# Threshold attention and GELU feed-forward on one core: score slots by query half, and the weight conversion's sign in a step of its own

## The chip, the cores and the metric

The kernel runs on one NeuronCore of a Trainium2 chip. The metric is the device time of one execution in microseconds (us). The five queues that matter are PE (matmul, with PEld for its weight loads), DVE (the vector engine), ACT (the scalar engine), POOL (GpSimd) and SP (issues nearly all DMAs).

## What is computed

Attention over 8 batches x 8 heads, 576 positions, head size 64, with a threshold per row, then a feed-forward block on the 4608 rows of 512 values:

```python
scores = scale * q @ k.T
thresh = max(scores, axis=-1) - tau
scores = where(scores >= thresh, scores, -1e9)
attn = exp(scores - max(scores)); attn /= sum(attn) + 1e-9
x = (attn @ v) rearranged to (B*S, H*D)
h = x @ w_in                      # 512 x 2048
out = (h / (1 + exp(-1.702 * h))) @ w_out   # 2048 x 512
```

The inputs q, k, v are float32. The two weight matrices arrive as float64, so the kernel makes float32 of them itself.

## The kernel before

**Pairs.** Two heads make a pair; there are 32 pairs, n = 0 to 31, four to a batch. The scores are kept transposed: keys on partitions, queries along the row. A pair has four main tiles of 128 keys for each head (t = 0 to 3) and one tail tile (t = 4) with the last 64 keys of both heads. `load_qk` and `load_v` (lines 183 to 207) bring q, k, v; `prep` (279) transposes q and k on DVE; `scores` (294) makes the scores of a tile on PE; `keep` (315) copies them from PSUM to an SBUF tile on ACT; `in_groups` (330) takes maxima over blocks on DVE; `over_tiles`, `over_groups`, `lower` and `spread_max` make the threshold of every query and spread it; `sub` (381) subtracts it on DVE; `mask` and `exps` (391, 395) follow on ACT; `values` (416) multiplies with v on PE; `sums_by_pe` (425, pairs 0 to 7) makes the denominators on PE, for later pairs DVE sums; `spread_sums` and `place_x` put the normalised result into `xT`.

**PSUM.** The pool `psA` has three slots of [128, 2, 512] float32. A main tile of scores takes two slots at once, one for each head; the two places in a slot hold the two halves of 288 queries. PE issues four matmul calls, half by half and head by head, each with 64 rows of the array; every call appears as two MATMUL records of 288 columns. Then two copies of [128, 576] follow, one for each head. The tail takes one slot, and so does `values`, from its start to `place_x`. The pool `psM` (two slots) serves the feed-forward block.

**Feed-forward.** Rows come in 9 blocks of 512. For each block there are 32 tasks `mm1` (line 490) and 32 tasks `mm2` (line 509), each two matmul calls, so four MATMUL records. `tanh` (ACT) and `gelu` (DVE, 501) follow every second `mm1`. Pair n may start its scores only after feed-forward task 16 (n - 6), so that the attention of later pairs runs among the feed-forward work of earlier ones.

**Weight conversion.** The weights come in 64 pieces of 128 x 256, 32 for w_in and 32 for w_out. `load_w` (215) issues two DMAs for a piece, the 64-bit words and the same bytes shifted by three. `cv_open` (233) is three DVE instructions: the fraction bits masked (239), the sign put into the fraction by an arithmetic shift and an exclusive or (243), the exponent field (248). `cv_mant` (254) turns the fraction into a float on ACT; `cv_exp` (259) clamps and shifts the exponent in two POOL instructions (262, 265); `cv_end` (269) multiplies both on POOL (272) and writes the float32 weight. The first feed-forward block waits for the pieces that each of its tasks reads.

**The order.** No engine chooses at run time. `run_in_order` (115) lists all tasks beforehand: each task has an engine, a cost in us, a rank, what it comes after, which buffers it takes and gives back, and a lag until others see its end. Whenever an engine is free, the ready task of lowest rank whose buffers are free goes next. The instructions are issued in that order, and the hardware then waits on semaphores with its own durations. Attention tasks of pair n have rank n, feed-forward matmuls 1000, `tanh`, `gelu` and the output tasks -1, conversion tasks 3.2 + i/64. The planner's costs and buffers for a piece are

```python
a = task("SP", 1.1, rank, load_w, i, take=("w64",), lag=3.5)
a = task("DVE", 1.0, rank, cv_open, i, after=[a], take=("cv",), give=("w64",))
m = task("ACT", 0.42, rank, cv_mant, i, after=[a])
e = task("POOL", 1.0, rank, cv_exp, i, after=[a])
ready_w.append(task("POOL", 0.9, rank, cv_end, i, after=[e, m], give=("cv",)))
```

with three buffers `w64` and two `cv`. For a main tile of scores they are 1.2 (PE), twice 0.64 (ACT, rank n) and 1.37 (DVE); a `mm1` or `mm2` costs 1.8, a `sub` 1.37, a `gelu` 0.7, `values` 5.0.

Of the kernel before, what the change touches and what calls it, by code (L numbers as in the profile page):

```python
# [9 lines left out]

FP32 = mybir.dt.float32
I32 = mybir.dt.int32
U32 = mybir.dt.uint32
U8 = mybir.dt.uint8
AF = mybir.ActivationFunctionType
ALU = mybir.AluOpType
# [3 lines left out]
P = 128  # L20
# [10 lines left out]
def kernel(  # L31
# [29 lines left out]
    nc = tc.nc  # L61
    B, H, S, D = q.shape
# [5 lines left out]
    SH = S // 2  # L68
# [11 lines left out]
    work = ctx.enter_context(tc.tile_pool(name="work", bufs=2))  # L80
    psA = ctx.enter_context(tc.tile_pool(name="psA", bufs=3, space=bass.MemoryType.PSUM))
# [6 lines left out]
    kd = [const.tile([P, P], FP32, name=f"kd{i}") for i in range(2)]  # L88
# [21 lines left out]
    def task(engine, cost, rank, f, *a, after=(), take=(), give=(), lag=0.06):  # L110
        tasks.append((engine, cost, rank, f, a, [x for x in after if x is not None],
                      take, give, lag))
        return len(tasks) - 1
# [57 lines left out]
    def home(n, tag, size, name, bufs, key=None):  # L171
        if n in APART:
            o = offset[key or tag]
            return spare[:, o : o + size]
        return work.tile([P, size], FP32, name=name, tag=tag, bufs=bufs)

    def own(n, *pools):
        return tuple(x + "_apart" for x in pools) if n in APART else pools
# [30 lines left out]
    WC = 256  # L209
# [3 lines left out]
    cv = {}  # L213
# [18 lines left out]

    def cv_open(i):
        t, t3 = cv[i]
        hi = t[:, :, 1]


        frac = work.tile([P, WC], I32, name="frac", tag="frac")
        nc.vector.tensor_scalar(  # L239
            out=frac, in0=t3[:, :, 0].bitcast(I32), scalar1=0x0FFFFFFF, scalar2=0x10000000,  # L240
            op0=ALU.bitwise_and, op1=ALU.bitwise_or,
        )
        nc.vector.scalar_tensor_tensor(  # L243
            out=frac, in0=hi.bitcast(I32), scalar=31, in1=frac,
            op0=ALU.arith_shift_right, op1=ALU.bitwise_xor,
        )
        ex = work.tile([P, WC], U32, name="ex", tag="ex")
        nc.vector.tensor_scalar(  # L248
            out=ex, in0=hi, scalar1=20, scalar2=0x7FF,
            op0=ALU.logical_shift_right, op1=ALU.bitwise_and,  # L250
        )
        cv[i] = [frac, ex]

    def cv_mant(i):
        mant = work.tile([P, WC], FP32, name="mant", tag="mant")
        nc.scalar.activation(out=mant, in_=cv[i][0], func=AF.Copy, scale=2.0**-28)  # L256
        cv[i][0] = mant

    def cv_exp(i):

        ex = cv[i][1]
        nc.gpsimd.tensor_scalar(  # L262
            out=ex, in0=ex, scalar1=1150.0, scalar2=896.0, op0=ALU.min, op1=ALU.max
        )
        nc.gpsimd.tensor_scalar(
            out=ex, in0=ex, scalar1=-896.0, scalar2=2.0**23, op0=ALU.add, op1=ALU.mult
        )

    def cv_end(i):
        dst, _, c, j = pieces[i]  # L270
        mant, ex = cv.pop(i)
        nc.gpsimd.tensor_tensor(  # L272
            out=dst[:, c, ts(j, WC)], in0=mant, in1=ex.bitcast(FP32), op=ALU.mult
        )


    mats, sT, stats, mbs, pss = {}, {}, {}, {}, {}
# [13 lines left out]
    def halves(ap):  # L291
        return ap.rearrange("p (c s) -> p c s", c=2)

    def scores(n, t):
        qT, kT = mats[n, 0], mats[n, 1]
        if t == NKT:
            ps = [psA.tile([P, 2, 512], FP32, name="ps", tag="ps")]
            for c in range(2):
                nc.tensor.matmul(  # L299
                    ps[0][:, c, 0:SH], lhsT=kd[n % 2], rhs=qT[:, ts(c, SH)],  # L300
                    start=True, stop=True,
                )
            del mats[n, 0], mats[n, 1]
        else:
            ps = [psA.tile([P, 2, 512], FP32, name="ps", tag="ps") for _ in range(2)]
            for c in range(2):
                for h in range(2):
                    nc.tensor.matmul(  # L308
                        ps[h][:, c, 0:SH],
                        lhsT=kT[ts(h, D), ts(t, P)], rhs=qT[ts(h, D), ts(c, SH)],  # L310
                        start=True, stop=True,
                    )
        pss[n, t] = ps

    def keep(n, t, h):
        ps = pss[n, t][h]
        if t == NKT:
            st = work.tile([P, S], FP32, name="s_t", tag="s_t", bufs=2)
            o = st
        else:  # L320
            if h == 0:
                st = home(n, "s_m", 2 * S, "s_m", 7, f"s_m{t}")
                st = st.rearrange("p (h s) -> p h s", h=2)
            else:
                st = sT[n, t]
            o = st[:, h, :]
        sT[n, t] = st
        nc.scalar.copy(out=halves(o), in_=ps[:, :, 0:SH])  # L328

    def in_groups(n, t, op):  # L330

# [186 lines left out]
    def store(blk, i):  # L518
# [6 lines left out]
        out=tau_b, in_=bass.AP(tensor=tau.tensor, offset=tau.offset, ap=[[0, P], [1, 1]])  # L525
# [23 lines left out]

    FIRST, LAST = -1.0, 1000.0
    BY_PE = 8
    LEAD = 6

    ready_w = []
    for i in range(len(pieces)):
        rank = NPAIR - 0.8 + i / len(pieces)
        if not wide:
            ready_w.append(task("SP", 0.6, rank, load_w, i, lag=2.5))  # L560
            continue
        a = task("SP", 1.1, rank, load_w, i, take=("w64",), lag=3.5)
        a = task("DVE", 1.0, rank, cv_open, i, after=[a], take=("cv",), give=("w64",))
        m = task("ACT", 0.42, rank, cv_mant, i, after=[a])
        e = task("POOL", 1.0, rank, cv_exp, i, after=[a])
        ready_w.append(task("POOL", 0.9, rank, cv_end, i, after=[e, m], give=("cv",)))

    tau_done = task("DVE", 1.0, -2.0, tau_terms)

# [41 lines left out]
    for n in range(NP):  # L611
        gate = per_pair * (n - LEAD)
        after = ffn[gate : gate + 1] if gate >= 0 else []
        r = float(n)
# [4 lines left out]
        pq = task("DVE", 0.78, r, prep, n, 0, after=[lq], take=own(n, "qkT0"), give=own(n, "raw0"))  # L619
        pk = task("DVE", 0.78, r, prep, n, 1, after=[lk], take=own(n, "qkT1"), give=own(n, "raw1"))  # L620
        pd = task("ACT", 0.5, r, prep_kd, n, after=[pk])
        mx = []
        for t in range(NKT + 1):
            tail = t == NKT
            a = task(
                "PE", 1.1 if tail else 1.2, r, scores, n, t,
                after=[pq, pk] + ([pd] if tail else []) + after,
                take=("psA", "s_t") if tail else ("psA", "psA") + own(n, "s_m"),
                give=own(n, "qkT0", "qkT1") if tail else (),
            )  # L630
            after = [a]
            c = [
                task("ACT", 0.64, r, keep, n, t, h, after=[a], give=("psA",))
                for h in range(1 if tail else 2)
            ]
            mx.append(task("DVE", 0.78 if tail else 1.37, r, in_groups, n, t, ALU.max, after=c))
        a = task("DVE", 0.75, r, over_tiles, n, ALU.max, after=mx)
        a = task("DVE", 0.75, r, over_groups, n, ALU.max, after=[a])
        a = task("DVE", 0.6, r, lower, n, after=[a, tau_done])
        m = task("DVE", 1.38, r, spread_max, n, after=[a], take=own(n, "mb"))  # L640
        ws, subs = [], [m]
        for t in range(NKT + 1):
            tail = t == NKT
            a = task(
                "DVE", 1.5 if tail else 1.37, r, sub, n, t, after=subs[-1:],
                give=own(n, "mb") if tail else (),
            )
            subs.append(a)
            a = task("ACT", 0.7 if tail else 1.17, r, mask, n, t, after=[a])
# [3 lines left out]
        if n < NPAIR:  # L653

            pv = den = None
            for t in every:
# [3 lines left out]
                    take=("psM", "psM") if first else (),  # L660
# [3 lines left out]
                    take=("psA",) if first else (), give=(back[t],) if t < NKT else ("s_t", "v_m"),  # L664
                )
            a = task("DVE", 1.2, r, one_row, n, after=[den], give=("psM", "psM"))
        else:
            pv = task("PE", 5.0, r, values, n, every, after=ws + [lv], take=("psA",), give=("v_m",))
        if NPAIR <= n < BY_PE:
            a = task("PE", 5.2, r, sums_by_pe, n, every, False, after=ws + [pv], take=("psA",), give=back)  # L670
            a = task("DVE", 1.2, r, one_row, n, after=[a], give=("psA",))
        elif n >= BY_PE:
# [4 lines left out]
            a = task("DVE", 0.75, r, over_tiles, n, ALU.add, after=su + [pv], give=back)  # L677
            a = task("DVE", 0.75, r, over_groups, n, ALU.add, after=[a])
            a = task("DVE", 0.7, r, one_group, n, after=[a])
        a = task("DVE", 1.05, r, spread_sums, n, after=[a])  # L680
# [41 lines left out]
```

## Time and profile before

| | us |
|---|---|
| median of three runs | 1481.49 |
| lowest, highest | 1479.97, 1481.97 |
| the profiled execution | 1479.97 |
| its span (first to last instruction) | 1478.2 |
| PE busy | 1417.4 (96%) |
| DVE busy | 988.5 (67%) |
| ACT busy | 662.2 (45%) |
| POOL busy | 113.2 (8%) |

The profile is one execution. Its parts are: the busy time of each engine; the span in 40 slices with the busy share of each engine in tenths; the DMA queues; the chain of waits that ended last, followed back from the end; and groups of instructions by line, engine and shape. A group's line gives its count after an x, then busy us and the mean ns of one, then the idle time of the engine just before them and what ended it. A timeline or the chain in order of time begins each line with the start in us and the length in us. A busy PE is not PE at its peak, since matmuls overlap.

### The profile page before, as it was taken

To read this page: it belongs to the slowest core of one execution; us is meant where nothing else is said; L and a number is where in the kernel's file an instruction comes from. 1 tells how busy PE (TensorE), PEld (TensorE's weight loads), DVE (VectorE), ACT (ScalarE), POOL (GpSimd) and SP (SyncE) were. 2 spreads that over 40 slices of the span, in tenths; PEclk is the share of its full clock that TensorE was granted. 3 is DMA by queue.
4 is the path that set the end of the run, shared out by engine and by line. 5 is a ranking of instruction groups with operands and counts; after the bars stand their busy time and mean duration, and the time that the engine had idled before them with its cause. 6 is when DMAs were issued, how large, how long until landed. Compare 5 with 4: busy or idle time off the path is not lost.

```text
span 1478.2 us, 14382 instructions
## 1 busy us (share of the span) xinstructions
PE 1417.4 (96%) x5056; PEld 661.5 (45%) x5056; DVE 988.5 (67%) x1678; ACT 662.2 (45%) x917; POOL 113.2 (8%) x204
## 2 busy tenths in 40 slices
PE   6888948999999999999999999999999999999998
PEld 3443414444444444444444444444444444444443
DVE  7989898448888888878788887888767840200200
ACT  6774443445544554555455555565444530100100
POOL 0127675000000000000000000000000000000000
PEclk9999979999999999999999999999999999999999
DMA  7236865210111111111111111111111000000000
GB/s 132 67 91 211 236 216 159 40 38 18 25 36 43 32 25 32 39 32 24 25 39 39 24 24 32 39 32 24 32 39 24 1 8 22 0 7 22 0 7 22
DMA packets 214296, 72.23 MB, mean 49 GB/s; under 512 B 193232, under 2 KB 201424, under 8 KB 214224
## 3 DMA queue, kind: packets, MB, share of 16 engines
q1 hardware_dynamic: 211856, 71.02, 19.7%
q8 instruction: 40, 0.66, 0.2%
q10 hardware_dynamic: 2368, 0.30, 0.2%
q14 instruction: 32, 0.26, 0.1%
HBM read 61.84 MB, written 9.44 MB: 48 GB/s over the span
## 4 chain that ended last, share of the span: by engine, by line
PE 82%; DVE 11%; DMA 2%; issue 2%; ACT 2%; SPq 0%; DVEq 0%; ACTq 0%
PE ops L509 31%; PE hps L490 30%; PE pv L411 9%; PE ps L308 8%; PE ps L299 2%; DVE frac L239 1%; DVE ex L248 1%; PE den L411 1%; DVE part L342 1%; DMA w64s<-in_moe_w_out_dram 1%; DVE s_m L384 1%; DVE frac L243 1%; DVE gT L501 1%; DVE s_t L387 0%; DVE qkT L282 0%
## 5 line engine op out<-in xcount | busy, mean ns | idle before, releaser
L509 PE MATMUL ops<-w_out,gT 128*128 128x512 f32 x1152 | 513.8, 600 | 22.4 <-POOL w_out L272 21.3
L490 PE MATMUL hps<-xT,w_in 128*128 128x512 f32 x1152 | 509.6, 596 | 4.9 <-DVE gT L501 4.2
L342 DVE TRANSPOSE_TENSOR_REDUCE part<-s_m 128x36 f32<-128x1152 f32 x216 | 290.3, 1361 | 111.7 <-ACT s_m L328 107.2
L509 PEld LDWEIGHTS ops<-w_out,gT 128*128 128x128 f32 x1152 | 215.8, 191 | 294.4 <-issue 259.5
L490 PEld LDWEIGHTS hps<-xT,w_in 128*128 128x128 f32 x1152 | 215.0, 190 | 273.8 <-issue 249.2
L328 ACT COPY s_m<-ps 128x576 f32<-128x576 f32 x240 | 142.0, 641 | 251.6 <-PE ps L308 251.4
L501 DVE SCALAR_TENSOR_TENSOR gT<-th,hps 128x512 f32<-128x512 f32 x144 | 96.7, 672 | 213.4 <-ACT th L498 212.8
L393 ACT ACTIVATE s_m<-s_m 128x1152 f32<-128x1152 f32 x120 | 138.3, 1153 | 71.6 <-DVE s_m L384 71.5
L498 ACT ACTIVATE th<-hps 128x512 f32<-128x512 f32 x144 | 84.9, 590 | 185.1 <-PE hps L490 185.1
L308 PE MATMUL ps<-qkT 64*128 64x288 f32 x960 | 154.3, 436 | 12.5 <-DVE qkT L282 10.0
L397 ACT ACTIVATE s_m<-s_m,shift,scl 128x1152 f32<-128x1152 f32 x120 | 161.3, 1344 | 2.8
L384 DVE TENSOR_TENSOR s_m<-s_m,mb 128x1152 f32<-128x1152 f32 x120 | 156.7, 1352 | 0.8
L308 PEld LDWEIGHTS ps<-qkT 64*128 64x128 f32 x960 | 86.5, 189 | 106.2 <-ACT s_m L328 37.7
L411 PE MATMUL pv<-s_m,v_m 128*64 128x288 f32 x960 | 125.7, 414 | 0.0
L516 ACT ACTIVATE osb<-ops 128x512 f32<-128x512 f32 x36 | 21.3, 592 | 211.4 <-PE ops L509 211.4
L411 PEld LDWEIGHTS pv<-s_m,v_m 128*64 128x64 f32 x960 | 67.7, 139 | 61.6 <-issue 7.6
L256 ACT ACTIVATE mant<-frac 128x256 f32<-128x256 int32 x64 | 26.2, 415 | 55.2 <-DVE frac L243 55.0
L282 DVE STREAM_TRANSPOSE qkT<-q_raw 128x576 f32<-128x576 f32 x30 | 23.3, 776 | 40.1 <-PE ps L299 36.7
L387 DVE TENSOR_TENSOR s_t<-s_t,mb 64x576 f32<-64x576 f32 x60 | 45.1, 752 | 0.4
L342 DVE TRANSPOSE_TENSOR_REDUCE part_t<-s_t 128x18 f32<-128x576 f32 x56 | 41.8, 747 | 1.4 <-ACT s_t L397 0.4
L376 DVE STREAM_TRANSPOSE mb<-thr 128x1152 f32<-128x1152 f32 x30 | 41.3, 1377 | 0.9
L262 POOL TENSOR_SCALAR ex<-ex 128x256 uint32<-128x256 uint32 x64 | 30.6, 477 | 120.9 <-DVE ex L248 119.4
(64 smaller groups left out, 754.1 us busy)
## 6 DMA issues: line engine op xcount, KB each, us to landing
out_dram<-osb SPq DMA_DIRECT2D x36, 256.0 KB, 2.0
q_raw<-in_q_dram SPq DMA_DIRECT2D x120, 72.0 KB, 2.4
k_raw<-in_k_dram SPq DMA_DIRECT2D x116, 72.0 KB, 2.4
v_m<-in_v_dram SPq DMA_DIRECT2D x64, 128.0 KB, 2.4
w<-in_moe_w_in_dram SPq DMA_DIRECT2D x32, 256.0 KB, 3.1
w<-in_moe_w_out_dram SPq DMA_DIRECT2D x32, 256.0 KB, 3.4
w64s<-in_moe_w_in_dram SPq DMA_DIRECT2D x32, 255.6 KB, 3.4
w64s<-in_moe_w_out_dram SPq DMA_DIRECT2D x32, 255.6 KB, 3.7
```

The lines of the kernel that those rows point to most:

```text
L308: nc.tensor.matmul(ps[h][:, c, 0:SH], lhsT=kT[ts(h, D), ts(t, P)], rhs=qT[ts(h, D), ts(c, SH)], start=True, stop=True,)
L328: nc.scalar.copy(out=halves(o), in_=ps[:, :, 0:SH])
L342: nc.vector.tensor_reduce(out=o, in_=i, axis=AXL.X, op=op, apply_transpose=True)
L384: nc.vector.tensor_tensor(out=s, in0=s, in1=mb, op=ALU.subtract)
L387: nc.vector.tensor_tensor(out=s[ts(h, D)], in0=s[ts(h, D)], in1=mb[ts(h, D), h, :], op=ALU.subtract)
L393: nc.scalar.activation(out=s, in_=s, func=AF.Prelu, alpha=STEEP)
L397: nc.scalar.activation(out=s, in_=s, func=AF.Exp, scale=scl, bias=shift)
L411: nc.tensor.matmul(o[c][ts(h, D), 0:SH], lhsT=lhsT, rhs=rhs, start=(t == 0), stop=(t == NKT),)
L490: nc.tensor.matmul(hidden[j], lhsT=w_in[:, c, ts(j, P)], rhs=xTs[blk][:, c, :], start=(c == 0), stop=(c == NDC - 1),)
L498: nc.scalar.activation(out=ths[j], in_=hidden[j], func=AF.Tanh, scale=GELU_SCALE / 2)
L501: nc.vector.scalar_tensor_tensor(out=gT[j], in0=ths.pop(j), scalar=1.0, in1=hidden.pop(j), op0=ALU.add, op1=ALU.mult)
L509: nc.tensor.matmul(acc[i], lhsT=gT[j][:, ts(i, P)], rhs=w_out[:, j, :], start=(j == 0), stop=(j == NFC - 1),)
```

## The change

Two things change, and the planner's tasks with them.

Conversion: `cv_open` loses the sign instruction and the setting of the hidden bit; it has two DVE instructions left, the mask and the exponent field. `cv_mant` adds 1.0 on ACT in place of the hidden bit. A new DVE step `cv_sign` takes the sign bit from the loaded words and joins it to the exponent that `cv_exp` has finished; `cv_end` comes after it. The load buffer `w64` is given back by `cv_sign`, no longer by `cv_open`.

Scores: a slot of `psA` holds both heads for one half of the queries. A main tile is two tasks on PE, each with two matmul calls (head 0 and head 1), and each takes one slot; each is followed by one copy of [128, 2, 288] that fills the same columns of both heads. The copies have rank -0.5, ahead of all attention work on ACT and behind `tanh` and the output copies.

```diff
--- before.py
+++ after.py
@@ -9,7 +9,6 @@
 from concourse.bass import ds, ts
 
 FP32 = mybir.dt.float32
-I32 = mybir.dt.int32
 U32 = mybir.dt.uint32
 U8 = mybir.dt.uint8
 AF = mybir.ActivationFunctionType
@@ -232,33 +231,26 @@
 
     def cv_open(i):
         t, t3 = cv[i]
-        hi = t[:, :, 1]
-
-
-        frac = work.tile([P, WC], I32, name="frac", tag="frac")
-        nc.vector.tensor_scalar(
-            out=frac, in0=t3[:, :, 0].bitcast(I32), scalar1=0x0FFFFFFF, scalar2=0x10000000,
-            op0=ALU.bitwise_and, op1=ALU.bitwise_or,
-        )
-        nc.vector.scalar_tensor_tensor(
-            out=frac, in0=hi.bitcast(I32), scalar=31, in1=frac,
-            op0=ALU.arith_shift_right, op1=ALU.bitwise_xor,
+        frac = work.tile([P, WC], U32, name="frac", tag="frac")
+        nc.vector.tensor_single_scalar(
+            out=frac, in_=t3[:, :, 0], scalar=0x0FFFFFFF, op=ALU.bitwise_and
         )
         ex = work.tile([P, WC], U32, name="ex", tag="ex")
         nc.vector.tensor_scalar(
-            out=ex, in0=hi, scalar1=20, scalar2=0x7FF,
+            out=ex, in0=t[:, :, 1], scalar1=20, scalar2=0x7FF,
             op0=ALU.logical_shift_right, op1=ALU.bitwise_and,
         )
-        cv[i] = [frac, ex]
+        cv[i] = [t, frac, ex]
 
     def cv_mant(i):
+
         mant = work.tile([P, WC], FP32, name="mant", tag="mant")
-        nc.scalar.activation(out=mant, in_=cv[i][0], func=AF.Copy, scale=2.0**-28)
-        cv[i][0] = mant
+        nc.scalar.activation(out=mant, in_=cv[i][1], func=AF.Copy, bias=1.0, scale=2.0**-28)
+        cv[i][1] = mant
 
     def cv_exp(i):
 
-        ex = cv[i][1]
+        ex = cv[i][2]
         nc.gpsimd.tensor_scalar(
             out=ex, in0=ex, scalar1=1150.0, scalar2=896.0, op0=ALU.min, op1=ALU.max
         )
@@ -266,9 +258,16 @@
             out=ex, in0=ex, scalar1=-896.0, scalar2=2.0**23, op0=ALU.add, op1=ALU.mult
         )
 
+    def cv_sign(i):
+        t, _, ex = cv[i]
+        nc.vector.scalar_tensor_tensor(
+            out=ex, in0=t[:, :, 1], scalar=0x80000000, in1=ex,
+            op0=ALU.bitwise_and, op1=ALU.bitwise_or,
+        )
+
     def cv_end(i):
         dst, _, c, j = pieces[i]
-        mant, ex = cv.pop(i)
+        _, mant, ex = cv.pop(i)
         nc.gpsimd.tensor_tensor(
             out=dst[:, c, ts(j, WC)], in0=mant, in1=ex.bitcast(FP32), op=ALU.mult
         )
@@ -291,41 +290,38 @@
     def halves(ap):
         return ap.rearrange("p (c s) -> p c s", c=2)
 
-    def scores(n, t):
+    def scores(n, t, c):
         qT, kT = mats[n, 0], mats[n, 1]
+        ps = psA.tile([P, 2, 512], FP32, name="ps", tag="ps")
         if t == NKT:
-            ps = [psA.tile([P, 2, 512], FP32, name="ps", tag="ps")]
-            for c in range(2):
+            for i in range(2):
                 nc.tensor.matmul(
-                    ps[0][:, c, 0:SH], lhsT=kd[n % 2], rhs=qT[:, ts(c, SH)],
+                    ps[:, i, 0:SH], lhsT=kd[n % 2], rhs=qT[:, ts(i, SH)],
                     start=True, stop=True,
                 )
             del mats[n, 0], mats[n, 1]
         else:
-            ps = [psA.tile([P, 2, 512], FP32, name="ps", tag="ps") for _ in range(2)]
-            for c in range(2):
-                for h in range(2):
-                    nc.tensor.matmul(
-                        ps[h][:, c, 0:SH],
-                        lhsT=kT[ts(h, D), ts(t, P)], rhs=qT[ts(h, D), ts(c, SH)],
-                        start=True, stop=True,
-                    )
-        pss[n, t] = ps
-
-    def keep(n, t, h):
-        ps = pss[n, t][h]
+            for h in range(2):
+                nc.tensor.matmul(
+                    ps[:, h, 0:SH],
+                    lhsT=kT[ts(h, D), ts(t, P)], rhs=qT[ts(h, D), ts(c, SH)],
+                    start=True, stop=True,
+                )
+        pss[n, t, c] = ps
+
+    def keep(n, t, c):
         if t == NKT:
             st = work.tile([P, S], FP32, name="s_t", tag="s_t", bufs=2)
-            o = st
+            o = halves(st)
         else:
-            if h == 0:
+            if c == 0:
                 st = home(n, "s_m", 2 * S, "s_m", 7, f"s_m{t}")
                 st = st.rearrange("p (h s) -> p h s", h=2)
             else:
                 st = sT[n, t]
-            o = st[:, h, :]
+            o = st[:, :, ts(c, SH)]
         sT[n, t] = st
-        nc.scalar.copy(out=halves(o), in_=ps[:, :, 0:SH])
+        nc.scalar.copy(out=o, in_=pss.pop((n, t, c))[:, :, 0:SH])
 
     def in_groups(n, t, op):
 
@@ -549,7 +545,8 @@
 
 
 
-    FIRST, LAST = -1.0, 1000.0
+
+    FIRST, COPY, LAST = -1.0, -0.5, 1000.0
     BY_PE = 8
     LEAD = 6
 
@@ -560,10 +557,11 @@
             ready_w.append(task("SP", 0.6, rank, load_w, i, lag=2.5))
             continue
         a = task("SP", 1.1, rank, load_w, i, take=("w64",), lag=3.5)
-        a = task("DVE", 1.0, rank, cv_open, i, after=[a], take=("cv",), give=("w64",))
+        a = task("DVE", 0.66, rank, cv_open, i, after=[a], take=("cv",))
         m = task("ACT", 0.42, rank, cv_mant, i, after=[a])
         e = task("POOL", 1.0, rank, cv_exp, i, after=[a])
-        ready_w.append(task("POOL", 0.9, rank, cv_end, i, after=[e, m], give=("cv",)))
+        a = task("DVE", 0.5, rank, cv_sign, i, after=[e], give=("w64",))
+        ready_w.append(task("POOL", 0.9, rank, cv_end, i, after=[a, m], give=("cv",)))
 
     tau_done = task("DVE", 1.0, -2.0, tau_terms)
 
@@ -622,18 +620,18 @@
         mx = []
         for t in range(NKT + 1):
             tail = t == NKT
-            a = task(
-                "PE", 1.1 if tail else 1.2, r, scores, n, t,
-                after=[pq, pk] + ([pd] if tail else []) + after,
-                take=("psA", "s_t") if tail else ("psA", "psA") + own(n, "s_m"),
-                give=own(n, "qkT0", "qkT1") if tail else (),
-            )
-            after = [a]
-            c = [
-                task("ACT", 0.64, r, keep, n, t, h, after=[a], give=("psA",))
-                for h in range(1 if tail else 2)
-            ]
-            mx.append(task("DVE", 0.78 if tail else 1.37, r, in_groups, n, t, ALU.max, after=c))
+            copies = []
+            for c in range(1 if tail else 2):
+
+                a = task(
+                    "PE", 1.1 if tail else 0.58, r, scores, n, t, c,
+                    after=[pq, pk] + ([pd] if tail else []) + after,
+                    take=("psA", "s_t") if tail else ("psA",) + (own(n, "s_m") if c == 0 else ()),
+                    give=own(n, "qkT0", "qkT1") if tail else (),
+                )
+                after = [a]
+                copies.append(task("ACT", 0.64, COPY, keep, n, t, c, after=[a], give=("psA",)))
+            mx.append(task("DVE", 0.78 if tail else 1.37, r, in_groups, n, t, ALU.max, after=copies))
         a = task("DVE", 0.75, r, over_tiles, n, ALU.max, after=mx)
         a = task("DVE", 0.75, r, over_groups, n, ALU.max, after=[a])
         a = task("DVE", 0.6, r, lower, n, after=[a, tau_done])
```

## The prediction

> **What bounds the kernel now.** I read the busy shares in 40 slices first, then the groups, the windows by stage, the chain of waits, and timelines of two stretches. The slices say that the span has two parts.
>
> ```profile
> PE   6888948999999999999999999999999999999998
> DVE  7989898448888888878788887888767840200200
> POOL 0127675000000000000000000000000000000000
> DMA  7236865210111111111111111111111000000000
> ```
>
> One slice is 37 us. POOL works in the first seven slices alone: it converts the weights. There PE has gaps and DVE has hardly any. From slice 8 PE is full. The windows by stage (busy us of PE, PEld, DVE, ACT, POOL, then granted clock, DMA share, GB/s) show the first part more closely.
>
> ```profile
> 112.00:160.00 48.00, 43.10 (x108) 18.30 (x109) 47.02 (x91) 24.83 (x42) 35.46 (x59) 1.00 0.65 206
> 180.00:224.00 44.00, 24.47 (x52) 8.82 (x50) 42.99 (x82) 22.45 (x37) 34.17 (x55) 0.74 0.66 212
> ```
>
> DVE is busy 47.0 of 48 and 43.0 of 44 us while PE is at 24.5 of 44. So up to the last converted piece the kernel goes at DVE's pace: 64 pieces of three DVE instructions each, mixed with the attention work of pairs 0 to 6. The groups for a piece (busy us, mean ns, idle before), and from the view of line 272 the minimum, median and maximum of the product on POOL and its first and last start:
>
> ```profile
> L243 DVE SCALAR_TENSOR_TENSOR frac<-w,frac 128x256 int32<-128x256 int32 x64 | 34.7, 541 | 2.2
> L248 DVE TENSOR_SCALAR ex<-w 128x256 uint32<-128x256 uint32 x64 | 29.2, 457 | 0.0
> L239 DVE TENSOR_SCALAR frac<-w64s 128x256 int32<-128x256 int32 x64 | 26.0, 406 | 10.8 <-DMA w64s<-in_moe_w_out_dram 6.1 <-DMA w64s<-in_moe_w_in_dram 2.7 <-ACT mant L256 1.8
> ```
>
> ```profile
> L272 POOL TENSOR_TENSOR w_out<-mant,ex x32: 722/730/1913, 172.8 to 250.3; 128x256 f32<-128x256 f32 x32
> ```
>
> The last product starts at 250.3; call that E. What PE has left at E takes 1478.2 - 250.3 = 1227.9 us, nearly without a gap. **The span is E plus PE's rest.** In that rest the chain of waits is PE alone:
>
> ```profile
> 434.96 1.17 PE ps L308 x8
> 436.13 1.91 PE ops L509 x4
> 438.05 1.17 PE ps L308 x8
> 439.22 1.17 PE ps L299 x4
> 440.38 18.88 PE ops L509 x44
> ```
>
> Columns: start, us, what. A feed-forward task in a long run takes 4 x 18.88/44 = 1.72 us, alone between two score groups 1.91. Eight score passes take 1.17 where pv's run at 5.00/40 = 0.125 each, so 1.00. An excursion of PE to the scores and back thus costs 0.19 + 0.17 = 0.36 us beyond the work.
>
> **What the Trainium skill says.** "TensorEngine Tiling (Array Packing)", section Key Properties: changing the tiling mode drains TensorE. The trace agrees; the price is the 0.36 us above for two changes. "SBUF — State Buffer", section Who interferes with whom: a VectorE instruction with two SBUF inputs contends with a GpSimd instruction that reads SBUF, and the later one blocks. It agrees too:
>
> ```profile
> 204.59 1.34 DVE L384 TENSOR_TENSOR s_m<-s_m,mb 128x1152 f32<-128x1152 f32 x1
> 204.61 1.91 POOL L272 TENSOR_TENSOR w_out<-mant,ex 128x256 f32<-128x256 f32 x1
> 205.86 0.81 DVE L239 TENSOR_SCALAR frac<-w64s 128x256 int32<-128x256 int32 x1
> ```
>
> The product takes 1.91 beside a subtraction, 0.73 otherwise (median above), and the DVE instruction behind it 0.81, not its median of 0.294 (view of its line). No third page is needed.
>
> **Conversion, the DVE work itself.** Three instructions go, 406 + 541 + 457 = 1404 ns. Three come: a mask (nearest row L239, 406), the exponent (457), and a sign step of L243's form (two SBUF inputs, 541). Difference 0. Bounds: L239's and L243's minima are 244 and 424, so up to (162 + 117) x 64 = 18 us less if the blocking of all of them went; I see no reason for that, and take 0, with 3 us either way.
>
> **Conversion, the order (+19).** The planner writes the order from its own costs. Before, a load slot (three of them) is held for 1.1 issue + 3.5 lag + 1.0 opening + 0.06 = 5.66; with half of a 1.37 attention step as wait on DVE, 6.35, so a piece every 2.1. Now it is held until the sign step: 1.1 + 3.5 + 0.66 + 0.06 + 1.0 (POOL) + 0.06 + 0.5 + 0.06 = 6.94, with two waits on DVE. Walked by hand, DVE's order becomes opening, one attention step, sign: 0.66 + 1.37 + 0.5 = 2.53 per piece for w_out, and with a gelu for every other piece 2.85 for w_in. Pieces 8 to 63 thus take 24 x 0.72 + 32 x 0.41 = 30 us more of planned time. Of that 56 x 0.16 = 9 is only the planner's dearer price for a piece (1.16, not 1.00), which the hardware doesn't pay. The rest, some 20, less what DVE can't fill, is attention work that now stands **ahead** of the last conversion: I take 19. Bounds 8 (loads hold less) and 30. SP's queue holds pair loads behind the later weight loads; they are due long before their use, so that costs nothing, and up to 2 us if pair 7's come late.
>
> **Conversion, the new wait (+7).** Behind the sign step on DVE stand the next opening and all attention steps; it waits for POOL's two exponent instructions. Beside a transposing maximum these are done in time (about 0.95 us within 1.37). Beside a subtraction they are blocked as shown, and start when it ends, so DVE waits 0.95. The 0.5 that L239 loses today behind a blocked product goes away. Some 15 subtractions (pairs 4, 5, 6) x 0.45 = 7. Bounds 0 and 14. POOL's product waits for the sign step too; only the next piece is behind it.
>
> **What comes back (-12).** With 19 us more of DVE attention done before E, pair 6 gets through its thresholds and pair 7 to its first maxima. PE then has pair 6's pv (4.90) and den (4.95) and two score groups (2.3) behind it: 12 us less in the rest. Bounds follow the 19: 5 to 20.
>
> **Scores.** PE executes the same 960 + 64 passes, two heads side by side, and ACT the same copies of 576 elements (641 ns). At the start, before DVE is the bound, four tiles go through a PE and copy cycle of 2.0 us where the maximum takes 1.36; the copy beside the next half takes out most of the difference, 4 x 0.64 = 2.6, less two transposes (0.75 each) that lay in those gaps: **-1.5**, bounds -3 and 0. The copies' rank puts them ahead of the previous pair's mask and exponent on ACT, which is busy 59 of 80 us from 20 to 100; up to 2 us late for pv, hidden by DVE, 0.
>
> In PE's full part the question is the number of excursions. I walked one pair of each kind by hand. Where a pair's first scores come before the last pair's pv (10 of pairs 8 to 31), PE asks for the third slot 0.15 us before the placement frees it, takes a feed-forward task as today, and nothing is saved. Where pv comes first (14 of them), tiles 2, 3 and the tail run together: one excursion less. Two late pairs, whose scores start after the placement, save about two more. (14 + 4) x 0.36 = **-6**. Bounds: -12 with one more per pair, +2 if the streamed halves wait on ACT (0.64 a copy against 0.5 a half).
>
> **Sum.** 19 + 7 - 12 - 1.5 - 6 = +6.5. The profiled execution took 1479.97 (span 1478.2, 1.8 around it), so 1486.5. It lies 1.5 below the median of 1481.49; on that scale 1488.
>
> **Rivals.** (A) The sum above, chance 0.45, own range 1485 to 1497. (B) Faster: the attention work moved ahead of E repays itself in full and DVE's wait is filled, so only PE's savings count: 1481.5 - 1.5 - 6 = 1474. For it: DVE is work-conserving, its work is unchanged. Against: E is later for PE's idle time too. It decides when E's delay less the repayment is under 7 us; chance 0.22. (C) The loads' ring binds: landing 3.7 + issue 0.8 + 0.86 + 1.15 + 0.54 + two waits of 0.7 = 8.5 a piece, 2.85 over three slots against 2.49 now (L248 at 112.2 for piece 8 and at 248.9 for piece 63, over 55); +20 without attention to fill, +7 blocking, -7.5: 1501, up to 1510. For it: DMA is at 0.98 in 160 to 180 us. Chance 0.18. (D) Both halves cancel: 1478.5 to 1484.5, chance 0.15.
>
> **How the numbers follow.** About 0.2% (3 us) can be told from no change here. Slower: A and C, 0.63; same: D, 0.15; faster: B, 0.22. The range leaves out half of B's lower side and the end of C: 1473 to 1506.
>
> **What would show it.** Right: the last w_out product near 275, not 250; POOL's exponent long beside subtractions and DVE waiting for it at the sign step; about 18 of PE's single feed-forward tasks between scores gone. Wrong: E within 10 us of 250 (B), or DVE idle by over 15 us in the conversion (C), or more feed-forward tasks alone between halves than before, 0.36 us for each.

## The result, and the profile after

| | before | after |
|---|---|---|
| median (us) | 1480.95 | 1491.57 |
| lowest, highest | 1479.97, 1481.97 | 1490.85, 1492.46 |
| profiled execution, its span | 1479.97, 1478.2 | 1492.46, 1490.7 |
| last w_out product starts (E) | 250.3 | 292.4 |
| PE's rest (span less E) | 1227.9 | 1198.3 |

The change makes the kernel slower: 1.0072 times the time before (95% interval 1.0054 to 1.0089). The time is inside the range and 3.6 us above the forecast of 1488.0. The direction holds, and so does the frame: the last piece comes later, part of that delay comes back, and PE changes its form less often. But two terms of the sum missed by far more than 3.6 us, in opposite directions; that they nearly cancel is luck.

The busy shares of after in 40 slices of 37 us:

```profile
PE   4688884799999999999999999999999999999998
DVE  6988778748888888877887688668867840110200
POOL 0016566400000000000000000000000000000000
DMA  6224775421111211210111111111111000000000
```

POOL's work now reaches into an eighth slice, and PE is full from slice 9. DVE is no longer full during the conversion: 7, 7, 8, 7, 4 where it had 8, 9, 8, 4, 4. The windows by stage of after (busy us of PE, PEld, DVE, ACT, POOL, then granted clock, DMA share, GB/s) say the same:

```profile
112.00:160.00 48.00, 41.53 (x184) 18.94 (x180) 37.56 (x78) 21.79 (x36) 28.68 (x44) 1.00 0.60 165
180.00:224.00 44.00, 40.24 (x154) 18.25 (x154) 34.24 (x78) 22.93 (x38) 28.10 (x45) 0.92 0.71 207
```

DVE is at 37.6 of 48 us and 34.2 of 44, where it was at 47.0 and 43.0. A stage that went at DVE's pace now leaves DVE idle for a fifth of its time. The groups of after by line and shape for a piece's DVE steps and its first exponent step on POOL (busy us, mean ns, idle before and what ended it), then the product from the view of its line:

```profile
L263 DVE SCALAR_TENSOR_TENSOR ex<-w,ex 128x256 uint32<-128x256 uint32 x64 | 29.6, 465 | 17.9 <-POOL ex L257 17.7
L235 DVE TENSOR_SCALAR frac<-w64s 128x256 uint32<-128x256 uint32 x64 | 21.5, 335 | 16.1 <-DMA w64s<-in_moe_w_out_dram 10.6 <-DMA w64s<-in_moe_w_in_dram 5.4
L239 DVE TENSOR_SCALAR ex<-w 128x256 uint32<-128x256 uint32 x64 | 19.8, 309 | 0.0
...
L254 POOL TENSOR_SCALAR ex<-ex 128x256 uint32<-128x256 uint32 x64 | 40.0, 625 | 113.2 <-DVE ex L239 110.5
```

```profile
L271 POOL TENSOR_TENSOR w_out<-mant,ex x32: 722/837/1705, 202.1 to 292.4; 128x256 f32<-128x256 f32 x32
```

Three readings. The sign step waits 17.7 us for POOL's second exponent step. The three DVE steps are busy 29.6 + 21.5 + 19.8 = 70.9 us, where the three of before took 34.7 + 29.2 + 26.0 = 89.9. And the last product starts at 292.4, 42.1 us later than before, and not at 275.

In PE's full part the chain of waits of after, in order of time, reads:

```profile
627.44 5.00 PE pv L407 x40
632.44 8.78 PE ops L505 x20
641.22 4.35 PE ps L305 x32
645.57 1.17 PE ps L298 x4
646.74 18.88 PE ops L505 x44
```

All four main tiles of a pair run as one: 32 passes in 4.35 us, with no feed-forward task between them. The pv of the pair before stands a stretch of feed-forward work, 8.8 us, ahead of them, which leaves time for its slot of `psA` to be given back. Before, every pair's four groups of 8 passes stood apart, most of them with one feed-forward task between two. Behind E, feed-forward tasks that stand alone between two score groups fall from 64 to 12. PE works in three forms here: 64x128 for the main score tiles, 128x64 for pv and den, 128x128 for everything else. A change from one form to another is called a mode change below. Behind E there are 222 of them before and 117 after.

What a mode change costs is worked out from the starts of PE's groups behind E: each group's time to the next group's start, less its passes at the price of long runs (0.429 us for a feed-forward record, 0.121 for a 64-row score record and for pv, 0.2425 for a tail record). It sums to 43.4 us before and 26.9 after, with any short wait of PE counted in. The 16.5 us saved over 105 changes are 0.16 each, near the half of 0.36 that the prediction used for one change.

### The profile page after: what moved, and what is told of

It is laid out like the page before. It is cut to its first block, busy times and chain, and to the rows that moved or that the text cites. A ratio compares the mean times of both kernels' runs of the same rounds, so it can differ in the third digit from the quotient of the medians.

```text
span 1490.7 us, 14379 instructions
## 1 busy us (share of the span) xinstructions
PE 1407.0 (94%) x5056; PEld 660.3 (44%) x5056; DVE 968.2 (65%) x1678; ACT 657.5 (44%) x917; POOL 119.8 (8%) x204
## 4 chain that ended last, share of the span: by engine, by line
PE 85%; DVE 7%; POOL 3%; DMA 2%; issue 1%; ACT 1%; SPq 0%; POOLq 0%; DVEq 0%; ACTq 0%
PE ops L505 33%; PE hps L486 31%; PE pv L407 10%; PE ps L305 8%; PE ps L298 2%; PE den L407 2%; DVE part L338 1%; POOL ex L254 1%; DMA w64s<-in_moe_w_out_dram 1%; DVE ex L263 1%; POOL ex L257 1%; POOL w_out L271 1%; DVE mb L372 1%; DMA w64s<-in_moe_w_in_dram 1%; DVE frac L235 0%
## 5 line engine op out<-in xcount | busy, mean ns | idle before, releaser
L338 DVE TRANSPOSE_TENSOR_REDUCE part<-s_m 128x36 f32<-128x1152 f32 x216 | 285.1, 1355 | 131.2 <-ACT s_m L324 129.9
L486 PEld LDWEIGHTS hps<-xT,w_in 128*128 128x128 f32 x1152 | 218.3, 191 | 282.1 <-issue 249.5
L324 ACT COPY s_m<-ps 128x576 f32<-128x576 f32 x240 | 135.8, 665 | 86.7 <-PE ps L305 85.9
L380 DVE TENSOR_TENSOR s_m<-s_m,mb 128x1152 f32<-128x1152 f32 x120 | 160.7, 1387 | 0.5
L305 PE MATMUL ps<-qkT 64*128 64x288 f32 x960 | 141.2, 437 | 15.1 <-DVE qkT L281 9.3
L305 PEld LDWEIGHTS ps<-qkT 64*128 64x128 f32 x960 | 81.5, 191 | 86.6 <-ACT s_m L324 31.4
L248 ACT ACTIVATE mant<-frac 128x256 f32<-128x256 uint32 x64 | 26.0, 415 | 65.1 <-DVE frac L235 65.0
L254 POOL TENSOR_SCALAR ex<-ex 128x256 uint32<-128x256 uint32 x64 | 40.0, 625 | 113.2 <-DVE ex L239 110.5
L407 PE MATMUL den<-s_m,ones 128*64 128x288 f32 x192 | 28.0, 437 | 17.5 <-ACT s_m L393 17.5
L338 DVE TRANSPOSE_TENSOR_REDUCE part_t<-s_t 128x18 f32<-128x576 f32 x56 | 42.1, 752 | 0.3
```

Source lines behind the costliest of these rows:

```text
L305: nc.tensor.matmul(ps[:, h, 0:SH], lhsT=kT[ts(h, D), ts(t, P)], rhs=qT[ts(h, D), ts(c, SH)], start=True, stop=True,)
L324: nc.scalar.copy(out=o, in_=pss.pop((n, t, c))[:, :, 0:SH])
L338: nc.vector.tensor_reduce(out=o, in_=i, axis=AXL.X, op=op, apply_transpose=True)
L380: nc.vector.tensor_tensor(out=s, in0=s, in1=mb, op=ALU.subtract)
L407: nc.tensor.matmul(o[c][ts(h, D), 0:SH], lhsT=lhsT, rhs=rhs, start=(t == 0), stop=(t == NKT),)
L486: nc.tensor.matmul(hidden[j], lhsT=w_in[:, c, ts(j, P)], rhs=xTs[blk][:, c, :], start=(c == 0), stop=(c == NDC - 1),)
```

## The experiments

Theories. **L, the load slot**: the planner sees `w64` held until the sign step, opens the pieces further apart, and puts attention between them. **W, the wait**: DVE stands at the sign step until POOL is done, and that spaces the pieces. **C**: the loads themselves are the limit. On the scores half, the question became why the first pieces come late; its theories are named where they come up. Each kernel's last product, its pace and its rest are taken from its own trace:

| | ratio to before (95%) | 8th product | pace after it | E | rest | mode changes' cost |
|---|---|---|---|---|---|---|
| before | 1 | 109.6 | 2.51 | 250.3 | 1227.9 | 43.4 |
| after | 1.0072 (1.0054–1.0089) | 122.2 | 3.04 | 292.4 | 1198.3 | 26.9 |
| e1 scores alone | 1.0030 (1.0019–1.0042) | 122.2 | 2.57 | 265.9 | 1217.0 | 29.9 |
| e2 conversion alone | 1.0094 (1.0080–1.0107) | 110.9 | 2.96 | 276.4 | 1215.5 | 43.2 |
| e3 after, copies at rank n | 1.0062 (1.0049–1.0075) | 121.6 | 3.02 | 291.0 | 1198.4 | 27.3 |
| e4 e1, copies at rank n | 1.0001 (0.9993–1.0009) | 118.8 | 2.59 | 263.6 | 1216.0 | 30.0 |
| e5 e2, sign ranked first | 1.0090 (1.0076–1.0104) | 107.5 | 3.00 | 275.4 | 1216.2 | 43.2 |
| e6 e2, four load slots | 1.0075 (1.0062–1.0089) | 111.4 | 2.72 | 263.5 | 1225.8 | 43.5 |
| e8 e2, sign planned later | 1.0158 (1.0144–1.0171) | 112.2 | 3.41 | 303.1 | 1198.3 | 42.4 |
| e9 halves from pair 5 | 0.9921 (0.9907–0.9935) | 108.8 | 2.55 | 251.5 | 1215.9 | 31.1 |
| e10 e1, early values later | 1.0019 (1.0012–1.0027) | 118.9 | 2.60 | 264.6 | 1216.0 | 29.9 |
| e11 e9, copies at rank n | 0.9916 (0.9901–0.9931) | 108.0 | 2.53 | 249.9 | 1215.6 | 30.8 |
| e12 conversion, halves from 5 | 0.9980 (0.9973–0.9988) | 111.9 | 2.95 | 276.9 | 1198.0 | 26.7 |
| e13 e1, early transposes first | 1.0011 (1.0004–1.0018) | 123.5 | 2.63 | 270.8 | 1212.0 | 29.1 |

The 8th product and E are starts in us. The pace is the time from the 8th to the 64th over 56, in us. Before as it was run beside each group had a median between 1480.89 and 1481.1 us.

### The two halves apart: e1 and e2

e1 takes the scores part of the diff alone, with its copies at rank -0.5; e2 takes the conversion part alone. Their cores:

```diff
     # e1, against before
-                take=("psA", "s_t") if tail else ("psA", "psA") + own(n, "s_m"),
+                    take=("psA", "s_t") if tail else ("psA",) + (own(n, "s_m") if c == 0 else ()),
...
     # e2, against before
-        a = task("DVE", 1.0, rank, cv_open, i, after=[a], take=("cv",), give=("w64",))
+        a = task("DVE", 0.66, rank, cv_open, i, after=[a], take=("cv",))
...
+        a = task("DVE", 0.5, rank, cv_sign, i, after=[e], give=("w64",))
```

> The score slots by query half with their copies at rank -0.5, and the weight conversion as before. Theory S (the conversion alone delays the last converted piece, the score slots save PE its mode changes): the last w_out product stays within 3 us of 250, PE's overhead behind it falls as in the changed kernel, so faster than before by 10 to 18 us, a ratio of 0.988 to 0.993. Rival R (the copies' rank delays mask and exponent of the early pairs, so that the score half delays the pieces too): last product at 258 to 268, time within 5 us of before or slower.

> The weight conversion with its sign step, and the score slots as before. Theory S: last w_out product at 285 to 295, as in the changed kernel, and slower than before by 22 to 30 us (42 us of delay less some 16 us of work that is moved ahead), ratio 1.015 to 1.020. Rival R: last product at 270 to 283, slower by 10 to 17 us.

Measured: e1 1484.57 us, e2 1494.67. E moves by 15.6 and by 26.1, together 41.7 of the 42.1 in after, so the two delays add. They come at different places: in e1 the 8th product is already 12.6 late and the pace hardly changes (2.57); in e2 the 8th is 1.3 late and the pace is 2.96. Behind E, e1 saves 13.5 us of mode changes and e2 alone next to none (222 changes, as before). So the saving belongs to the scores half, though 3.0 of the 16.5 us in after come only with both halves. Both came as rival R on record had it; its reason in e1, the copies' rank, is tried in e4. From the view of the product's line, e1 and then e2:

```profile
L272 POOL TENSOR_TENSOR w_out<-mant,ex x32: 724/730/1243, 185.6 to 265.9; 128x256 f32<-128x256 f32 x32
```

```profile
L272 POOL TENSOR_TENSOR w_out<-mant,ex x32: 724/733/1709, 188.8 to 276.4; 128x256 f32<-128x256 f32 x32
```

DVE's waits in e2 from 110 to 280 us (us in total, times, longest):

```profile
DVE ex L264 <- POOL ex L258: 17.6, 30, 1.0
DVE frac L236 <- DMA w64s<-in_moe_w_out_dram: 6.5, 6, 1.7
...
DVE frac L236 <- DMA w64s<-in_moe_w_in_dram: 1.6, 3, 0.9
```

DVE waits for POOL 30 times, but for loads only 6.5 + 1.6 = 8.1 us; before, the group of the mask had 6.1 + 2.7 = 8.8. In e2 DVE thus waits no longer for loads than before, which speaks against C. In after those waits are 10.6 + 5.4 = 16.0; there C has up to 7 us.

### What sets the pace: e5, e6, e8

All three start from e2. e5 ranks the sign step ahead of all attention on DVE. e6 gives the loads a fourth slot (the shifted bytes keep three buffers); the float mantissa is written over the fraction to make room for it. e8 leaves the hardware alone and only tells the planner that POOL's exponent takes 2.0.

```diff
     # e5
-        a = task("DVE", 0.5, rank, cv_sign, i, after=[e], give=("w64",))
+        a = task("DVE", 0.5, -0.6, cv_sign, i, after=[e], give=("w64",))
...
     # e6
-        t = work.tile([P, WC, 2], U32, name="w64", tag="w64", bufs=3)
+        t = work.tile([P, WC, 2], U32, name="w64", tag="w64", bufs=4)
...
     # e8
-        e = task("POOL", 1.0, rank, cv_exp, i, after=[a])
+        e = task("POOL", 2.0, rank, cv_exp, i, after=[a])
```

> The conversion of the changed kernel with the old score slots, and the sign step at rank -0.6, so that the planner puts it next on DVE once the exponent is done. Theory L (the planner spaces the pieces by how long a load slot is held): the hold gets shorter only where the sign step stood behind other DVE work of lower rank, so the last product comes 0 to 8 us earlier than 276. Rival W (DVE's in-order wait for POOL at the sign step sets the pace): no change or later, since the sign step stands as close behind the exponent as before.

> The same kernel (conversion of the changed kernel, old score slots) with four load slots for the 64-bit words and not three; to make room, the mantissa is written over the fraction. Theory L: the planned hold of about 8.3 us over four slots is 2.1 a piece, as before the change, so the last product comes back to 252 to 264 and the time to within 6 us of before. Rival W: DVE still waits at every sign step, so the last product stays at 270 or later.

> The same kernel with three slots, and the planner told that the exponent step takes 2.0 us and not 1.0, so that one more DVE step stands ahead of the sign step. DVE's wait for POOL at the sign step (18 us in all) should fall under 5 us. Theory L: the slot is held 1 us longer, a third of that for each of 56 pieces: the last product at 285 to 298, and slower. Rival W: the last product falls to 260 to 268.

Measured: 1494.18, 1492.24 and 1504.03 us. The lines of the product, e6 and then e8:

```profile
L272 POOL TENSOR_TENSOR w_out<-frac,ex x32: 718/839/1847, 179.3 to 263.5; 128x256 f32<-128x256 f32 x32
```

```profile
L272 POOL TENSOR_TENSOR w_out<-mant,ex x32: 723/845/1822, 198.6 to 303.1; 128x256 f32<-128x256 f32 x32
```

The sign step of e8 (busy us, mean ns, DVE's idle time before it and what ended it):

```profile
L264 DVE SCALAR_TENSOR_TENSOR ex<-w,ex 128x256 uint32<-128x256 uint32 x64 | 30.9, 486 | 6.1 <-POOL ex L258 5.8
```

e8 moves E by 26.7 through the order alone, while DVE's wait for POOL at the sign step falls from 18.7 us in e2 to 5.8. e6 takes 12.9 of the 26.1 back with that wait still there (17.7). So the planned order sets the pace, and W isn't what spaces the pieces, though its 18 us are real. e5 tells nothing apart: E moved by 1.0.

That the load slot is what stretches the order (L) is shown for about half of the delay. Under L, e6 was to bring E to 252 to 264 and the time within 6 us of before. E comes to 263.5, half of the way back to 250.3, and the time stays 11.3 above. For the other half a rival is **not tried**: the two `cv` buffers of a piece are held from its opening to its product, and the sign step now lies in between. e8 lengthens both holds, and no run gives `cv` a third buffer.

A fourth slot would also help under C, so against C stand the load waits of e2 and e8, not e6. In e8 those waits grow by 6.1 us, to 8.6 + 5.6, while E moves by 26.7.

Little time follows E. In e6, E is 12.9 earlier and the rest 10.3 longer, so the time gains 2.4, which isn't clear of noise. In e8, E is 26.7 later and the rest 17.2 shorter, so the time loses 9.4. Attention done ahead of the last piece is attention that PE doesn't do behind it.

### The copies' rank: e3, e4, e11

```diff
-                copies.append(task("ACT", 0.64, COPY, keep, n, t, c, after=[a], give=("psA",)))
+                copies.append(task("ACT", 0.64, r, keep, n, t, c, after=[a], give=("psA",)))
```

e3 is after with this line, e4 is e1 with it, e11 is e9 (below) with it.

> The changed kernel with one edit: the score copies have their pair's rank again, not -0.5. Theory S: DVE has other work while pv waits, so nothing before 110 us changes: piece 8 is still done near 124 us and the time within 4 us of the changed kernel. Rival R: piece 8 comes back to about 114 us, the last product to 280 to 285, and the time falls by 5 to 10 us against the changed kernel.

> The score slots by query half, the conversion as before, and the copies at their pair's rank. Theory S: the same as the score slots alone with rank -0.5, within 3 us. Rival R: faster than that by 5 us or more, since the early pairs are no longer held up; last product at 246 to 252.

> The faster version (old conversion, halves from pair 5 on) with the copies at their pair's rank. In the later pairs ACT has room: within 2 us of 1469.2 if the rank matters in the early pairs alone; faster or slower by 3 us or more if it also shapes the order of the late ones.

Measured: 1490.62, 1481.32 and 1468.80 us. Against its own base, e4 gains 3.3 us, e3 1.0 and e11 0.4; the last two are within what can be told from no change. In e4 the 8th product comes 3.4 earlier, so the rank costs something in the early pairs, a quarter of the 12.6 and not the rest of it.

### Where the early delay sits: e9, e12

e9 is e1, but pairs 0 to 4 keep the old slots and the old copies. e12 is the same with the new conversion.

```diff
+            if n < 5:
+                a = task(
+                    "PE", 1.1 if tail else 1.2, r, scores_whole, n, t,
...
+                    take=("psA", "s_t") if tail else ("psA", "psA") + own(n, "s_m"),
```

> The old conversion; pairs 0 to 4 keep a slot for each head, pairs 5 to 31 have slots by query half with copies at rank -0.5. Theory V (in the early pairs the single slots let pv and den of the pair ahead go between the scores, so that DVE gets its maxima late; in the later pairs they only save mode changes): the last product returns to 248 to 254 and PE's overhead behind it falls by 12 to 16 us, so 1464 to 1470 us, a ratio of 0.988 to 0.993. Rival: what delays the pieces are the score halves of pairs 5 and 6, beside the conversion: last product at 258 to 266 and the time within 4 us of before.

> The conversion of the changed kernel with halves from pair 5 on. If the two halves of the change are independent once the early pairs are as before, the conversion's cost of 13.6 us stands on the faster version: 1481 to 1485 us, last product at 274 to 280. If they interact (the streamed scores also fill what the slower conversion leaves), it costs under 9 us: 1472 to 1478.

Measured: e9 1469.17 us, e12 1477.93. The product's line in e9, and a stretch of its chain of waits:

```profile
L272 POOL TENSOR_TENSOR w_out<-mant,ex x32: 724/727/1914, 172.7 to 251.5; 128x256 f32<-128x256 f32 x32
```

```profile
623.07 5.00 PE pv L444 x40
628.07 1.17 PE ps L342 x8
629.24 1.91 PE ops L542 x4
631.15 1.17 PE ps L342 x8
632.33 1.91 PE ops L542 x4
634.24 2.18 PE ps L342 x16
636.42 1.17 PE ps L335 x4
```

E is back at 251.5 and the 8th product at 108.8, so the early delay of e1 belongs to pairs 0 to 4. The rest is 12.0 shorter than before, and mode changes account for it with 12.3: this is the scores half's gain without its cost. All that was expected of e9 came, but the reason given, values between the early scores, is only tried in e10.

The chain also shows where part of the gain is not had. Here the pv comes right ahead of the scores and holds one of the three slots, so two single feed-forward tasks still stand between the score groups, and only the last two tiles run as one. Of the 25 pairs behind E in e9, 11 look like this, and 11 run all four tiles as one. In after, where attention is about a pair further ahead, it is 4 and 17 of 24. So there are 117 mode changes there and 146 in e9.

In e12 the conversion costs 1477.93 - 1469.17 = 8.8 us on top of e9, with E later by 25.4 and the rest shorter by 17.9. On top of before it cost 13.6 (e2). Of the 4.8 between them, 4.4 are mode changes (31.1 in e9, 26.7 in e12): attention pushed ahead saves them only where the halves are in use.

### Why the first pieces are late: e10, e13

Two theories, both tried on e1. In e10, values of pairs 0 to 3 take slots between the halves of the next pair's tiles, so their rank is raised. In e13 (theory G), score groups run closer together at the start, and the next pair's q and k transposes, ranked behind, wait for the whole DVE chain of the pair before; so the transposes of early pairs go first.

```diff
     # e10
-                    "PE", 1.1, r, values, n, [t], after=[ws[t], den, pv, lv],
+                    "PE", 1.1, r + 1.5, values, n, [t], after=[ws[t], den, pv, lv],
...
     # e13
+        rp = r - 1.5 if n <= NPAIR else r
-        pq = task("DVE", 0.78, r, prep, n, 0, after=[lq], take=own(n, "qkT0"), give=own(n, "raw0"))
+        pq = task("DVE", 0.78, rp, prep, n, 0, after=[lq], take=own(n, "qkT0"), give=own(n, "raw0"))
```

> The old conversion and slots by query half for all pairs, with one edit: the value products of pairs 0 to 3 have the rank of their pair plus 1.5, so they come behind the next pair's scores, as they did before the change. Theory V (a single free slot lets the value product of the pair ahead in before the next pair's scores, and DVE gets its maxima late): piece 8 back from 122 to 108 to 114 us, the last product to 250 to 257, and 7 to 13 us faster than the score slots alone, so 1471 to 1478. Rival C (the copies themselves, by halves, hold up the early pairs): piece 8 stays at 118 or later and the time within 4 us of 1484.6.

> The old conversion and slots by query half for all pairs (the score slots alone), with one edit: the q and k transposes of pairs 0 to 4 on DVE have the rank of their pair less 1.5, so that they come ahead of the previous pair's DVE work. Theory G (the gaps between the maxima, which the score halves closed, were where the next pair's transposes went; without them the transposes wait behind the previous pair's whole DVE chain, its scores start late, and DVE stands idle afterwards): pair 1's scores start before 22 us and not at 32, piece 8 is back at 106 to 113 us, the last product at 247 to 256, and the time at 1464 to 1473, as with the old slots in the early pairs. Rival C (halved copies on ACT hold up the early pairs): piece 8 stays at 118 or later and the time within 4 us of 1484.6.

Measured: e10 1483.80 us, the 8th product at 118.9; e13 1482.78, the 8th at 123.5. Windows of DVE alone (busy us, granted clock, DMA share, GB/s) for 24 to 45 us, of before, of e1 and of e13:

```profile
24.00:45.00 21.00, 19.91 (x31) 0.84 0.54 141
```

```profile
24.00:45.00 21.00, 15.71 (x26) 0.86 0.59 126
```

```profile
24.00:45.00 21.00, 17.82 (x30) 0.84 0.45 111
```

In e1 DVE stands idle for 5.3 of these 21 us, where before it did for 1.1. Up to 125 us it does 100.6 us of work, 7.3 less than the 107.9 of before. This is G's idle time: pair 1's scores start at 32 in e1, at 18.3 before. e13 brings them to 16.8 and DVE back to 105.5. But the pieces don't come earlier. Their openings end with the exponent field, which starts at 98.6 for the first piece of e13, at 32.1, 33.2, 79.7, 80.7, 108.1, 109.1 and 119.0 for the first seven of e1, and at 37.7, 59.9, 60.9, 81.0, 82.0, 100.9 and 101.8 before. The values' rank (e10) is worth 3.3 us of the 12.6 at the 8th product and fell as the cause. G explains the idle time and not the pieces. Their rank of 3.2 puts them behind pairs 0 to 3, so they get what DVE time those pairs leave, and which ready task closes the gaps that before had left to pieces is **not settled**. Both runs came out as the rival on record had it, that the halved copies on ACT hold up the early pairs. No run tries those copies alone, so that rival stands.

## Why the prediction was right or wrong

**E and the rest.** The frame held: span = E plus rest in every kernel, with PE full behind E.

**Conversion, the order (+19) and the new wait (+7).** Together 26; e2 has 26.1. The parts are different. Overlaps counted once, DVE's time up to E in e2 is 20.5 us less conversion, 30.2 more of other work, and 16.4 more idle. So the moved attention was at the upper bound of 30, and the idle time above the bound of 14; that the sum of the two terms is right to 0.1 is luck, since both came out larger and the 20.5 us of DVE work that went make up for it. The step on the wait said 7 from 15 subtractions; the sign step waits 30 times, 17.6 us. One sum of the walk is slightly off: half a gelu of 0.7 makes 2.53 into 2.88 a piece, not 2.85.

**Conversion, the DVE work (0).** This step failed. The prediction named the 18 us that would go if all of the blocking went, and saw no reason for it. The groups lost 19.0 us. Sorted by what POOL does beside them, the mean beside a product falls from 556 to 371 ns for the mask, which also lost its OR, and from 643 to 305 for the exponent field, the same instruction in both, while with POOL idle both take 271 to 286 ns, before and after. The Trainium skill, "SBUF — State Buffer", section Who interferes with whom, says that GpSimd and a VectorE instruction that reads two SBUF inputs use the same ports, and that this is an exclusive lock. The trace agrees: the sign step, the one with two SBUF inputs, takes 726 ns beside a product and 419 alone. Before, that instruction stood between the other two and 19 of 64 ran beside a product; now it stands alone and 9 do. All seven kernels with the old conversion have 618 to 714 ns for the exponent field beside a product, and all seven with the new one 304 to 334, whatever their score slots. So the conversion half is the cause; that it is the place of the sign step is argued from these means and wasn't tried by itself.

**What comes back (-12).** The size is right: e2's rest is 12.4 shorter. PE has 40 records of pv, 40 of den and 36 of scores more ahead of E than before. These are pair 6's pv and den, as the step said, and all of pair 7's scores, where it said two groups of 8.

**Scores, the start (-1.5).** This step failed, in sign too. E is 15.6 later in e1. The prediction saw that PE, copies and maxima would run closer together and counted the time between a pair's own tiles. It priced the two transposes in those gaps at 0.75 each, and didn't ask who waits for them: pair 1's scores start at 32 in e1, at 18.3 before. Nor did it ask what the weight pieces would get, and why they come late stays open. The step's sum is off too: 2.6 less two transposes is 1.1, not 1.5. Nothing of this delay comes back: e1's rest is 10.9 shorter, less than its 13.5 of mode changes.

**The copies' rank (0).** Off by 3.3 us in e4, by 1.0 in e3.

**Mode changes (-6).** The mechanism is right, the size is too small: -16.5 in after, -13.5 in e1. The walk by hand allowed 14 + 4 excursions fewer; feed-forward tasks alone between score groups fell by 52. It took the pairs' timing as it was: 10 pairs with scores ahead of the last pv, where nothing is saved, and 14 where the last two tiles and the tail run together. Behind E in after, 2 of 24 pairs have scores ahead of the pv, and 17 run all four tiles together, with the pv a stretch of feed-forward work ahead. The bound of +2, halves that wait on ACT, didn't come: 32 x 0.121 = 3.88, and the 0.47 that are left in 4.35 are about one excursion.

**Sum.** Predicted +24.5 for E and -18 behind it, +6.5. Measured +42.1 and -29.6, +12.5 in the profiled executions and +10.6 in the medians. The start was 17 short, the mode changes 10.5 short the other way, so the sum came near by luck.

**The rivals.** B (1474) is not what happened, since the delay of E isn't repaid in full. C said 2.85 us a piece (its 8.5 over three is 2.83) where after has 3.04, and the idle DVE that was to be its sign is there (61.2 us up to E, 29.4 before). Its cause isn't: the same loads went at 2.51 a piece before, and slow from 2.96 in e2 to 3.41 in e8 by the order alone. D needed a sum near zero.

**The best version.** e11 (1468.80) and e9 (1469.17) can't be told apart. They keep the old conversion, and the old slots for pairs 0 to 4: 0.8% under before, and 1.5% under after.

## What to carry to other kernels

Where the order is written out ahead from planned costs, one more step in a chain that holds buffers changes the whole order, so walk the planner with every new hold before adding up instructions. A delay of the stage that ends early is not a loss of that size: of e2's 26.1 us nearly half came back. A half that gains late and loses early can be applied late only, and here that was worth more than either kernel.

## What was not expected of the hardware

The exponent field is the same one-input instruction on 128 x 256 integers in both kernels. It takes 457 ns on average where it follows the step with two SBUF inputs, and 309 where it doesn't; with POOL idle it takes 286 and 283. POOL's first exponent step went the other way, from a mean of 477 to 625 ns. A mode change of PE costs 0.16 us over the whole of its full part, and 105 fewer of them were worth 16.5.
